# Turning k' with 128-row products against an identity instead of 64-row transposes

## The chip, the cores and the metric

One core of a Trainium2 chip. The sets of runs were on different chips, each with the kernel before in the same rounds. The metric is the device time of the whole kernel in microseconds, the median over several executions. The profile gives, for one execution, the span from the first to the last instruction, which is about 1.8 us shorter than the time. PE is the matrix engine (TensorE), PEld its weight loads, DVE VectorE, ACT ScalarE, POOL GpSimd.

## The reference

Linear attention with projected keys and values (8 batches, 8 heads, 1024 tokens, head width 64, projection to 64), followed by a gated feed-forward block on all 8192 tokens:

```python
k_proj = np.einsum('ks,bhsd->bhkd', E, k)
v_proj = np.einsum('ks,bhsd->bhkd', F, v)
scores = scale * np.matmul(q, k_proj.transpose(0, 1, 3, 2))
attn = softmax(scores)                      # over 64 projected keys
x = np.matmul(attn, v_proj)                 # gathered to (8192, 512)
g = x @ w_gate                              # 512 -> 1536
out = (g * sigmoid(g) * (x @ w_val)) @ w_out
```

## The kernel before

The feed-forward matmuls of batch b are the frame; the attention of the next batch is put into slots between them. In the profiles gps, vps and yps are the PSUM tiles of its gate, value and output products, kvp holds the projected k and v, kTp the turned k', sc the scores; `64*128` behind MATMUL or LDWEIGHTS is the tile of the PE array, rows times columns, that the instruction uses. The change touches one small stage: the projected k of a batch, k' (64 rows of projected keys, 8 heads x 64), comes out of PSUM into `ks`, is turned so that the head width lies on partitions, and is written into the block-diagonal `BD` from which the scores are computed.

```python
def u_KV(b, what="kv", hs=(0, H), at="a"):
    ...                                   # t[0:64] = E k, t[64:128] = F v
    if "k" in what:
        if (b, "s") not in kvp:
            kvp[b, "s"] = aw.tile([KP, H, D], BF16, name="ks", tag="ks")
        nc.scalar.copy(out=kvp[b, "s"][:, h0:h1], in_=t[0:64, h0:h1])
    ...

def u_KT(b, at="a", prs=(0, NPAIR)):
    ks = kvp[b, "s"]
    t = bank(at, [P, NPAIR, KP], BF16, "kTp")
    for pr in range(*prs):                # four pairs of heads
        nc.tensor.transpose(
            out=t[:, pr, :],
            in_=ks[:, 2 * pr : 2 * pr + 2, :].rearrange("p h d -> p (h d)"),
            identity=ident_bf[:KP, :KP],
        )
    bd = BD[b % 2][:].rearrange("p (a c) k -> p a c k", c=2)
    for c in range(2):
        src = t[64 * c : 64 * c + 64, slice(*prs)]
        nc.vector.tensor_copy(out=bd[0:64, slice(*prs), c, 0:64], in_=src)
        nc.vector.tensor_copy(out=bd[64:128, slice(*prs), c, 64:128], in_=src)
```

Each of batches 1 to 7 has one such visit of four transposes, in the middle of the feed-forward matmuls of the batch ahead of it. Batch 0 has two visits of two, in the opening, where nothing else is there to be computed yet:

```python
u_KV(0, "k", (0, 4), at="y"); warm(1)
u_T(0, 0, "a", act)
u_KT(0, at="v", prs=(0, 2))
...
u_S(0, 0, "g"); u_R(0, 0); u_N(0, 0)       # scores, sums, scaling (on POOL)
load_w_gv(1, 2, (1,))                      # weight loads, issued by POOL in this order
...                                        # the second half of k', more scores and scalings
load_w_gv(2, 4)                            # later weights, behind the scalings on POOL
```

The softmax here doesn't subtract the row's maximum and nothing guards it: scores larger than these inputs give would overflow.

## Time and profile before

| | before |
|---|---|
| time | 571.42 us, median of 3 (571.02 to 571.66) |
| span of the profiled run | 569.4 us |
| PE busy | 562.6 us, 99% |
| DVE busy | 335.2 us, 59% |
| PE's waits from 40 us on | none |

PE carries the kernel. Since its instructions overlap, busy time does not tell how densely they stand; what counts is the distance from one start to the next.

### The profile page before, as it was taken

To read this page: it belongs to the slowest core of one execution; us is meant where nothing else is said; L and a number is where in the kernel's file an instruction comes from. 1 tells how busy PE (TensorE), PEld (TensorE's weight loads), DVE (VectorE), ACT (ScalarE), POOL (GpSimd) and SP (SyncE) were. 2 spreads that over 40 slices of the span, in tenths; PEclk is the share of its full clock that TensorE was granted. 3 is DMA by queue.
4 is the path that set the end of the run, shared out by engine and by line. 5 is a ranking of instruction groups with operands and counts; after the bars stand their busy time and mean duration, and the time that the engine had idled before them with its cause. 6 is when DMAs were issued, how large, how long until landed. Compare 5 with 4: busy or idle time off the path is not lost.

```text
span 569.4 us, 7879 instructions
## 1 busy us (share of the span) xinstructions
PE 562.6 (99%) x2939; PEld 266.7 (47%) x2939; DVE 335.2 (59%) x577; ACT 236.8 (42%) x417; POOL 109.1 (19%) x122
## 2 busy tenths in 40 slices
PE   8999999999999999999999999999999999999997
PEld 5654444444444444444444444444444444444444
DVE  4776664766476655666466655666546665545550
ACT  4565442454435433443435434354343543443222
POOL 6742250124002400124002230023100220000000
PEclk9999999999999999999999999999999999999999
DMA  9999979829903696039931399105990213010002
GB/s 211 179 199 198 167 131 201 141 60 205 198 18 75 108 177 141 37 56 158 189 79 38 75 178 207 41 20 104 191 185 20 57 38 75 37 38 37 20 37 94
DMA packets 111143, 62.91 MB, mean 110 GB/s; under 512 B 64256, under 2 KB 102400, under 8 KB 111104
## 3 DMA queue, kind: packets, MB, share of 16 engines
q0 software_dynamic: 42800, 29.36, 36.3%
q1 hardware_dynamic: 67392, 31.46, 25.6%
q10 hardware_dynamic: 912, 1.57, 0.9%
q8 instruction: 23, 0.38, 0.3%
q14 instruction: 16, 0.13, 0.1%
HBM read 60.29 MB, written 16.78 MB: 135 GB/s over the span
## 4 chain that ended last, share of the span: by engine, by line
PE 92%; DMA 3%; DVE 2%; POOL 1%; ACT 1%; issue 0%; ACTq 0%; DVEq 0%; POOLq 0%
PE yps L362 29%; PE vps L324 28%; PE gps L324 27%; PE kvp L149 3%; PE sc L229 2%; PE pv L287 2%; DMA wv<-in_moe_w_val_dram 2%; DMA kraw<-in_k_dram 1%; DVE zz L244 1%; POOL AA L260 0%; POOL wg L117 0%; DVE hT L348 0%; ACT xT L137 0%; DVE s L343 0%; PE kTp L174 0%
## 5 line engine op out<-in xcount | busy, mean ns | idle before, releaser
L343 DVE SCALAR_TENSOR_TENSOR s<-th,gps 128x512 f32<-128x512 f32 x192 | 130.5, 679 | 143.1 <-ACT th L336 143.0
L324 PE MATMUL gps<-xT,wg 128*128 128x512 bf16 (+1 forms) x776 | 197.8, 377 | 0.6 <-DMA wg<-in_moe_w_gate_dram 0.4
L324 PE MATMUL vps<-xT,wv 128*128 128x512 bf16 (+1 forms) x776 | 197.5, 377 | 0.1
L362 PE MATMUL yps<-wo,hT 128*128 128x512 bf16 (+1 forms) x780 | 194.5, 376 | 0.0
L336 ACT ACTIVATE th<-gps 128x512 f32<-128x512 f32 x192 | 114.6, 597 | 157.9 <-PE gps L324 156.4
L348 DVE TENSOR_TENSOR hT<-s,vps 128x512 bf16<-128x512 f32 x192 | 132.0, 688 | 20.0
L260 POOL TENSOR_TENSOR AAd<-ee,rr 128x512 bf16<-128x512 f32 x56 | 58.3, 1041 | 343.3 <-issue 157.2
L362 PEld LDWEIGHTS <-hT 128*128 128x128 bf16 x780 | 76.2, 98 | 89.9
L324 PEld LDWEIGHTS <-wv 128*128 128x128 bf16 x776 | 73.9, 98 | 83.9 <-issue 3.3
L324 PEld LDWEIGHTS <-wg 128*128 128x128 bf16 x776 | 73.9, 98 | 82.1 <-issue 1.0
L372 ACT ACTIVATE ysb<-yps 128x512 f32<-128x512 f32 (+1 forms) x65 | 38.4, 591 | 76.7 <-PE yps L362 76.7
L137 ACT CAST xT<-pv 128x512 bf16<-128x512 f32 x63 | 36.6, 585 | 51.0 <-PE pv L287 50.1
L244 DVE TENSOR_REDUCE zz<-ee 128x8 f32<-128x512 f32 x64 | 43.4, 679 | 21.8 <-ACT ee L233 21.8
L233 ACT ACTIVATE ee<-sc 128x512 f32<-128x512 f32 x64 | 37.9, 595 | 23.6 <-PE sc L229 22.3
L229 PEld LDWEIGHTS <-qTd 128*128 128x128 bf16 x224 | 17.2, 98 | 13.2
L287 PE MATMUL pv<-AT,BDV 128*128 128x512 bf16 x60 | 22.4, 379 | 0.0
L229 PE MATMUL sc<-BD,qTd 128*128 128x128 bf16 x224 | 21.6, 219 | 0.0
L137 DVE CAST BDV<-kvp 64x256 bf16<-64x256 f32 x14 | 6.0, 426 | 20.0 <-ACT ks L159 17.8
L246 DVE RECIPROCAL rr<-zz 128x8 f32<-128x8 f32 x64 | 13.0, 203 | 7.4 <-DVE zz L244 1.4
L149 PE MATMUL kvp<-vb,FT 128*64 128x512 bf16 (+2 forms) x80 | 15.6, 338 | 0.3 <-ACT BDV L137 0.3
L149 PE MATMUL kvp<-kb,ET 128*64 128x512 bf16 (+1 forms) x72 | 15.5, 357 | 0.5 <-DMA kb<-in_k_dram 0.3
L107 POOL DMA_DIRECT2D qb<-in_q_dram x17 | 15.6, 919 | 0.6 <-DMA wv<-in_moe_w_val_dram 0.6
(51 smaller groups left out, 126.3 us busy)
## 6 DMA issues: line engine op xcount, KB each, us to landing
out_dram<-ysb SPq DMA_DIRECT2D x63, 256.0 KB, 2.4
qb<-in_q_dram POOLq DMA_DIRECT2D x15, 512.0 KB, 18.2
kb<-in_k_dram POOLq DMA_DIRECT2D x7, 1024.0 KB, 11.0
vb<-in_v_dram POOLq DMA_DIRECT2D x7, 1024.0 KB, 14.4
wo<-in_moe_w_out_dram POOLq DMA_DIRECT2D x2, 768.0 KB, 21.8
wg<-in_moe_w_gate_dram POOLq DMA_DIRECT2D x5, 256.0 KB, 9.5
wv<-in_moe_w_val_dram POOLq DMA_DIRECT2D x5, 256.0 KB, 10.1
kraw<-in_k_dram ACTq DMA_DIRECT2D x2, 512.0 KB, 4.7
```

What stands on the lines that cost most here:

```text
L137: (nc.scalar.copy if eng is nc.scalar else eng.tensor_copy)(out=out, in_=in_)
L149: nc.tensor.matmul(out=t[lo : lo + 64, h0:h1].rearrange("p h d -> p (h d)"), lhsT=w[:, j, :], rhs=src[b][:, h0:h1, j, :], start=(j == 0), ...
L229: nc.tensor.matmul(out=ps[:, n, :], lhsT=t[:, n, :], rhs=BD[b % 2][:, 4 * g + n, :], start=True, stop=True)
L233: nc.scalar.activation(out=e[:].rearrange("p h j k -> p (h j k)"), in_=ps[:].rearrange("p a k -> p (a k)"), func=AF.Exp, scale=scale,)
L244: nc.vector.reduce_sum(out=z[:], in_=e[:], axis=AX.X)
L260: eng.tensor_tensor(out=a.rearrange("p j h k -> p h j k"), in0=ee.pop((b, u))[:], in1=rr.pop((b, u))[:].unsqueeze(3).to_broadcast([P, 4, 2 ...
L324: nc.tensor.matmul(out=ps[:, ts], lhsT=(wg, wv)[w][:, kt, f * P : (f + 1) * P], rhs=x[:, kt, ts], start=(kt == 0), stop=(kt == NKT - 1),)
L336: nc.scalar.activation(out=th[:], in_=ps[:], func=AF.Tanh, scale=0.5)
L343: nc.vector.scalar_tensor_tensor(out=s1[:], in0=th[:], scalar=1.0, in1=g[:], op0=ALU.add, op1=ALU.mult)
L348: nc.vector.tensor_tensor(out=hT[c][:, f, :], in0=s1[:], in1=ps[:], op=ALU.mult)
L362: nc.tensor.matmul(out=yy[c][:, cs], lhsT=hT[c][:, f, i * P : (i + 1) * P], rhs=wo[:, f, cs], start=(f == 0), stop=(f == NFT - 1),)
L372: nc.scalar.activation(out=ysb[:, cs], in_=yy[c][:, cs], func=AF.Copy, scale=0.5)
```

## The change

The intent: take the 64-row operation out of the stream of 128-row ones. `ks` gets 128 rows, of which the lower 64 are zero, and the turn becomes an ordinary product with an identity, which writes fp32.

```diff
+    ks = [const.tile([P, H, D], BF16, name=f"ks{i}") for i in range(2)]
...
-            if (b, "s") not in kvp:
-                kvp[b, "s"] = aw.tile([KP, H, D], BF16, name="ks", tag="ks")
-            nc.scalar.copy(out=kvp[b, "s"][:, h0:h1], in_=t[0:64, h0:h1])
+            nc.scalar.copy(out=ks[b % 2][0:64, h0:h1], in_=t[0:64, h0:h1])
...
-        t = bank(at, [P, NPAIR, KP], BF16, "kTp")
+        t = bank(at, [P, NPAIR, KP], FP32, "kTp")
         for pr in range(*prs):
-            nc.tensor.transpose(
+            nc.tensor.matmul(
                 out=t[:, pr, :],
-                in_=ks[:, 2 * pr : 2 * pr + 2, :].rearrange("p h d -> p (h d)"),
-                identity=ident_bf[:KP, :KP],
+                lhsT=ks[b % 2][:, 2 * pr : 2 * pr + 2, :].rearrange("p h d -> p (h d)"),
+                rhs=ident_bf[:, 0:KP],
+                start=True,
+                stop=True,
             )
...
         for i in range(2):
+            nc.vector.memset(ks[i][64:P], 0.0)
```

More of the change, by code (lines that the diff above doesn't have):

```diff
@@ L169, in u_KT @@
     def u_KT(b, at="a", prs=(0, NPAIR)):
-        ks = kvp[b, "s"]
-        t = bank(at, [P, NPAIR, KP], BF16, "kTp")
+        t = bank(at, [P, NPAIR, KP], FP32, "kTp")
         for pr in range(*prs):
-            nc.tensor.transpose(
+            nc.tensor.matmul(
                 out=t[:, pr, :],
-                in_=ks[:, 2 * pr : 2 * pr + 2, :].rearrange("p h d -> p (h d)"),
-                identity=ident_bf[:KP, :KP],
+                lhsT=ks[b % 2][:, 2 * pr : 2 * pr + 2, :].rearrange("p h d -> p (h d)"),
+                rhs=ident_bf[:, 0:KP],
+                start=True,
+                stop=True,
             )
```

## The prediction

> **What bounds the kernel now.** I read the page first, then the list of waits of the matrix engine, then the timeline of that engine and of its weight loads around one of the places that the diff touches, then the groups by shape and the timeline of the opening. The page's first block and its chain come first:
>
> ```profile
> PE 562.6 (99%) x2939; PEld 266.7 (47%) x2939; DVE 335.2 (59%) x577; ACT 236.8 (42%) x417; POOL 109.1 (19%) x122
> ...
> PE 92%; DMA 3%; DVE 2%; POOL 1%; ACT 1%; issue 0%; ACTq 0%; DVEq 0%; POOLq 0%
> ```
>
> PE is busy 99% of the 569.4 us span, and 92% of the chain that ended last is PE. A busy PE is not yet a PE at its peak, so I asked what it waits for: in the list of PE's own waits there are eight entries, 1.2 us at most, all in the first 33 us; from 40 us to the end the list is empty. The granted clock is 0.999. So after the opening the time is the sum of what PE takes for its instructions in order. Only two things can move it: a matmul's own spacing, or a pause between matmuls that the list of waits does not name. The second is what this change is after. The timeline of PE at batch 2 (start us, length us, engine, line, operation, tile, count):
>
> ```profile
> 101.26 1.03 PE L362 MATMUL yps<-wo,hT 128*128 128x512 bf16 x4
> 102.22 0.29 PE L174 MATMUL kTp<-ident_bf,ks 64*128 64x64 bf16 x4
> 102.44 1.04 PE L324 MATMUL gps<-xT,wg 128*128 128x512 bf16 x4
> 103.32 1.03 PE L324 MATMUL vps<-xT,wv 128*128 128x512 bf16 x4
> 104.18 1.03 PE L362 MATMUL yps<-wo,hT 128*128 128x512 bf16 x4
> 105.04 0.39 PE L229 MATMUL sc<-BD,qTd 128*128 128x128 bf16 x4
> 105.27 0.38 PE L324 MATMUL gps<-xT,wg 128*128 128x512 bf16 x1
> ```
>
> Read starts, not lengths, since lengths overlap. A block of four 512-column matmuls takes 0.86 us when 128-row work follows (103.32 to 104.18, 104.18 to 105.04). The block ahead of the transposes takes 0.96 (101.26 to 102.22). The weight loads of the same stretch show why:
>
> ```profile
> 102.22 0.17 PEld L174 LDWEIGHTS <-ks 64*128 64x128 bf16 x4 [0.42 <-issue]
> 102.44 0.55 PEld L324 LDWEIGHTS <-wg 128*128 128x128 bf16 x4
> 103.10 0.75 PEld L324 LDWEIGHTS <-wv 128*128 128x128 bf16 x4
> ...
> 104.83 0.42 PEld L229 LDWEIGHTS <-qTd 128*128 128x128 bf16 x4
> ```
>
> The score weights (tile 128*128) are loaded at 104.83, 0.21 us ahead of their matmul at 105.04. The ks weights (tile 64*128) are not loaded ahead, they start with their matmul at 102.22, and so do the wg weights after them, at 102.44. At each change of the array's tile the load-ahead is lost.
>
> **What the Trainium skill says.** TensorEngine Tiling (Array Packing), Key Properties: "Changing tiling mode (not just tile) drains the TensorE". The trace agrees: the pause stands at 64*128 and not at the score block. PSUM — Partial Sum Buffer, Specifications (TRN2): TensorE writes fp32, except that transposes write the input's type; VectorE takes 0.52 ns an element when both sides are 2-byte, otherwise 1.04. So the change of the tile from bf16 to fp32 is forced, and the trace agrees on what it costs: in the groups by shape, copies of 64x256 out of bf16 take 284 to 289 ns, out of fp32 426.
>
> ```profile
> L137 DVE CAST BDV<-kvp 64x256 bf16<-64x256 f32 x14 | 6.0, 426 | 20.0 <-ACT ks L159 17.8 <-PE kvp L149 2.2
> L183 DVE COPY BD<-kTp 64x256 bf16<-64x256 bf16 x14 | 4.0, 289 | 0.2
> L183 DVE COPY BD<-kTp 64x128 bf16<-64x128 bf16 x4 | 0.9, 222 | 0.1
> ```
>
> TensorE: Matmul & The Clock Gate, LDWEIGHTS: a load's time goes with its columns, not its rows. The trace has 95 ns for 64 rows of 128 columns and 98 ns for 128 rows, so the zero lower half costs nothing to load. Perfetto Trace Analysis, Transposes, advises a real transpose over a standard matmul; that speaks against the change, and the trace shows nothing for or against it.
>
> **The change part by part.** The instructions on PE stay equal in number and order; there is no extra matmul.
>
> 1. The seven steady visits (batches 1 to 7, four transposes each). Before, one visit costs, beyond plain blocks: 0.96 - 0.86 = 0.10 ahead of it, 102.22 to 102.44 = 0.22 for the four and the pause behind them, and 0.02 because the next block takes 0.88 (102.44 to 103.32) rather than 0.86. Sum 0.34 us. I read four more visits (159.82, 227.77, 363.68, 431.63 us): 0.96 ahead, 0.21 to 0.22 within, each. After, the four are 64-column matmuls with no change of tile. Inside the visit now, four starts lie within 0.29 - 0.19 = 0.10 us (0.19 is one's length in the groups), so 0.033 apart; four at that spacing take 0.13. The score block, 128 columns, runs at 0.055 (0.22 for four), the worst case. Saving 0.34 - 0.13 = 0.21 us a visit, at worst 0.12; by seven, 1.5 us, at worst 0.8. All of it lies on the path, since PE waits for nothing there.
>
> 2. The four copies out of that tile on DVE: 426 rather than about 287 ns, 0.14 x 4 = 0.56 us a visit, 3.9 us of DVE busy in all. They lie beside PE. At batch 2 they run from 102.63 to 103.83; DVE then sits idle 0.32 us until 104.15. After, they end near 104.4, the next two eviction steps come 0.25 late, and an idle of 0.53 us follows before the next reduction. The score matmuls that read BD started at 105.04 and would come about 0.2 sooner, at 104.84: 0.4 us to spare, the tightest of the visits (there the scores start 2.8 us behind kTp, at batch 3 3.7 us). No cost to the end.
>
> 3. Two memsets of 64x256 words on DVE, some 0.27 each by the BDV memset of the same width (272 ns). DVE sits idle 1.6 us for the first k load there. Hidden.
>
> 4. The opening, batch 0, where k' is turned in two halves. The first is on a chain through scores, exponential, sums, scaling:
>
> ```profile
> 9.48 0.23 PE L174 MATMUL kTp<-ident_bf,ks 64*128 64x64 bf16 x2
> ...
> 10.46 0.23 DVE L183 COPY BD<-kTp 64x128 bf16<-64x128 bf16 x1
> 10.55 0.34 PEld L229 LDWEIGHTS <-qT 128*128 128x128 bf16 x4
> 10.55 0.52 PE L229 MATMUL sc<-BD,qT 128*128 128x128 bf16 x4
> ```
>
> The last copy ends at 10.69, inside the score block, which therefore takes 0.52 and not 0.39. A copy of 64x128 is 222 ns; from fp32 I estimate 222 + 128 x (426 - 287)/256 = 290. Four: +0.27 us, less about 0.1 as the drain ahead of kTp goes. So +0.17 there. In the second half the neighbour ahead is a turn of F in the 64*128 tile, so there the change of tile only moves from behind to ahead of kTp, and the four copies push the copies of AT and qT behind them by 0.27. But the opening ends with PE ahead of its weights: blocks at 31.89 and 33.21 us waited 0.5 and 0.2 us for loads of wg and wv, and the chain there is a transfer of 10 us with the DMA engines at 90% and more. Up to 0.7 us of delay on PE vanishes in it; only if the loads, issued behind the scaling on POOL, come late too, is 0.2 to 0.3 paid. I take +0.15.
>
> Sum: -1.5 + 0.15, rounded down a little for spacing: -1.25 us. 571.42 - 1.25 = 570.2.
>
> **The rivals.** (a) The pause does not come from the 64-row tile but from transposing, or from the first matmul on a new bank. Against it: the 128-row transposes of q in the second half of batch 0 (34.09 to 34.31) take 0.22 for four, with no extra. Were it so, nothing is saved and the opening's cost stays: 571.4 to 571.7. (b) The score matmuls come to wait for the slower copies, 0.4 us to spare at batch 2 by my count; a miss of 0.2 at one visit costs 0.2. DVE at 59% busy does not become the bound. (c) The opening's delay goes through in full, to the weight loads: +0.5 at most, 570.5. (d) Pauses ahead of and behind kTp vanish wholly and 64-column matmuls run at their shortest: 0.24 by seven, 1.7 us: 569.7. (e) Plain matmuls are paced slower than transposes, as the score block: 570.8.
>
> **Range and chances.** From (d) with a little of chance to (e) with the opening's cost and the 0.6 us that three runs of before lie apart: 569.5 to 571.3. A gain of 2% would be 11.4 us; all kTp visits together cost 7 x 0.34 = 2.4 us, so that is out of reach, and so is a loss of 2%, which would take a wait of 1.6 us at every visit. Hence 0.99 for within 2%, 0.0 for faster, and 0.01 for slower, kept for what I have not thought of.
>
> **What would show it right or wrong.** The timeline at batch 2: kTp as tile 128*128, 0.86 from the block ahead, 0.11 to 0.14 for the four; their weights loaded 0.2 us ahead of the first; the issue wait gone from the list for that line (3.0 us over 7 visits now). Copies of 64x256 at some 426 ns and no new entry in PE's waits after 40 us. If kTp still starts 0.96 after its block, step 1 is wrong and (a) holds; if the visits shrink but the time does not, the opening took it: compare the start of the first block after 33 us. A prediction fails outright if a score block waits for BD by name.

## The result, and the profile after

The changed kernel takes 570.19 us (median of 6, 569.91 to 571.33) where the kernel before takes 571.47 us (median of 6 with those of the same rounds). The ratio is 0.9981, with a 95% interval from 0.9968 to 0.9994: about 0.2% faster, within 2%, and clear of 1. Such a ratio is the mean time of one kernel's runs over that of the other's of the same rounds, so it is not quite the ratio of the two medians. In means the gain is 1.10 us, in medians 1.28 us. That difference is already a sign of how finely this can be timed: single runs of one kernel lie 0.6 to 1.4 us apart.

The page of the changed kernel opens with this:

```profile
PE 561.2 (99%) x2939; PEld 266.8 (47%) x2939; DVE 339.9 (60%) x579; ACT 236.7 (42%) x417; POOL 109.1 (19%) x122
```

As many PE instructions as before, 2939, and two DVE instructions more, the memsets; DVE is 4.7 us busier. The timeline of PE at the same visit, batch 2, in the changed kernel (start us, length us, engine, line, operation, tile, count):

```profile
101.66 1.03 PE L365 MATMUL yps<-wo,hT 128*128 128x512 bf16 x4
102.53 0.28 PE L175 MATMUL kTp<-ident_bf,ks 128*128 128x64 bf16 x4
102.64 1.03 PE L327 MATMUL gps<-xT,wg 128*128 128x512 bf16 x4
103.50 1.03 PE L327 MATMUL vps<-xT,wv 128*128 128x512 bf16 x4
104.37 1.03 PE L365 MATMUL yps<-wo,hT 128*128 128x512 bf16 x4
105.23 0.39 PE L232 MATMUL sc<-BD,qTd 128*128 128x128 bf16 x4
```

The block ahead of kTp now takes 0.87 us from its start to the start of kTp (0.96 before), the four products take 0.11 us (0.22), the block behind them 0.86 (0.88). From the start of the yps block to the start of the next yps block it is 2.71 us, and it was 2.92. The timeline of the weight loads of the same stretch shows the cause:

```profile
101.45 0.75 PEld L365 LDWEIGHTS <-hT 128*128 128x128 bf16 x4
102.31 0.37 PEld L175 LDWEIGHTS <-ks 128*128 128x128 bf16 x4
102.61 0.56 PEld L327 LDWEIGHTS <-wg 128*128 128x128 bf16 x4
```

The first ks load now starts at 102.31, 0.22 us ahead of its product at 102.53, under the last matmul of the block before. No `issue` wait (time in which the engine waited for nothing that the profile shows) stands at this line any more; before, the seven visits had 3.0 us of them on PEld (which is not the same as PE time: most of such a wait lies beside a running matmul).

The groups by shape of the changed kernel, for the copies out of the turned tile (mean ns before the last bar):

```profile
L186 DVE CAST BD<-kTp 64x256 bf16<-64x256 f32 x14 | 5.9, 423 | 0.2
L186 DVE CAST BD<-kTp 64x128 bf16<-64x128 f32 x4 | 1.2, 289 | 0.1
```

They cost 423 and 289 ns where they cost 289 and 222 ns out of bf16. At batch 2 the four end 2.23 us behind the start of kTp and the score block starts 2.70 us behind it, so 0.47 us remain.

To split the gain by stage I take starts that both profiles share. From the last feed-forward block ahead of the first visit to the first one behind the seventh, the time was 376.32 us (from 55.53 to 431.85) and is 374.86 us (from 56.14 to 431.00): 1.46 us less, 0.21 us for each of seven visits. From there to the start of the last run of yps matmuls (554.51 and 553.65) it is 122.7 us in both. The rest of the difference lies ahead of 56 us and is of the other sign: in these two profiles the first visit's block came 0.61 us later. How much of that belongs to the change is the subject of half of the experiments.

### The profile page after: what moved, and what is told of

Read it like the earlier page. It is cut to its first block, busy times and chain, and to the rows that moved or that the text cites. A ratio compares the mean times of both kernels' runs of the same rounds, so it can differ in the third digit from the quotient of the medians.

```text
span 568.5 us, 7881 instructions
## 1 busy us (share of the span) xinstructions
PE 561.2 (99%) x2939; PEld 266.8 (47%) x2939; DVE 339.9 (60%) x579; ACT 236.7 (42%) x417; POOL 109.1 (19%) x122
## 4 chain that ended last, share of the span: by engine, by line
PE 92%; DMA 3%; POOL 2%; ACT 1%; DVE 1%; issue 0%; POOLq 0%; DVEq 0%
PE yps L365 29%; PE vps L327 28%; PE gps L327 27%; PE kvp L150 3%; PE sc L232 2%; PE pv L290 2%; DMA wv<-in_moe_w_val_dram 2%; DMA kb<-in_k_dram 2%; POOL AA L263 0%; DVE zz L247 0%; POOL wg L118 0%; ACT xT L138 0%; POOL qb L108 0%; POOL wv L118 0%; ACT th L339 0%
```

## The experiments

Theory: a 64-row operation among 128-row ones costs PE a fixed pause ahead of and behind it, because the load of the next weights is not done ahead across the change of tile; everything else that the change touches lies beside PE, but for the copies in the opening. Rivals: that the gain comes from product instead of transpose, or from the storage; that the pause grows with the number of transposes and not of tile changes; that the slower copies are not really hidden; and, for the opening, that its later end is only chance of when weights land.

Time differences below are between the means of the runs, against the kernel before in the same rounds.

| kernel | batches 1 to 7 | batch 0 | median us | mean against before, us |
|---|---|---|---|---|
| the change (three times) | 128-row product | same | 570.19, 570.35, 570.32 | -1.10, -1.04, -1.21 |
| e3_prod64 | 64-row product | same | 571.71 | +0.27 |
| e2b_t128_full | 128-row transpose, bf16 | same | 570.53 | -0.78 |
| e6_storage | 64-row transpose, bf16 | same | 571.41 | -0.01 |
| e4_split_before | as before, two visits of two | as before | 573.03 | +1.60 |
| e5_split_after | 128-row product, two visits of two | 128-row product | 569.87 | -1.50 |
| e8_copies_twice | 128-row product, copies twice | 128-row product | 574.39 | +2.58 |
| e1_open_old (twice) | 128-row product | 64-row transpose, bf16 | 569.87, 570.14 | -1.58, -1.23 |
| e9_open_t128 | 128-row product | 128-row transpose, bf16 | 570.31 | -1.24 |
| e10_open_copies_twice | 128-row product | 128-row product, copies twice | 573.25 | +1.74 |

All gave the right result.

### Rows or product: e3_prod64, e2b_t128_full and e6_storage

Product over the 64 rows that hold data, into fp32:

```diff
-                lhsT=ks[b % 2][:, 2 * pr : 2 * pr + 2, :].rearrange(...),
-                rhs=ident_bf[:, 0:KP],
+                lhsT=ks[b % 2][0:KP, 2 * pr : 2 * pr + 2, :].rearrange(...),
+                rhs=ident_bf[:KP, 0:KP],
```

> Products into an fp32 tile as in the change, but over the 64 rows that hold data. Theory (rows make the pause): 0.96 us ahead of kTp and 0.22 us within stay in every visit, and the opening's slower copies are paid without the gain: 571.5 to 572.1. Rival (product instead of transpose makes the gain): 570.2 as the change.

Transposes over 128 rows, into bf16. In transpose mode the check ahead of the chip takes only a whole permutation as the moving operand, so the identity is 128 x 128, and each transpose has 128 columns:

```diff
-        t = bank(at, [P, NPAIR, KP], FP32, "kTp")
+        t = bank(at, [P, NPAIR, P], BF16, "kTp")
-            nc.tensor.matmul(..., rhs=ident_bf[:, 0:KP], start=True, stop=True)
+            nc.tensor.transpose(..., identity=ident_bf[:])
-            src = t[64 * c : 64 * c + 64, slice(*prs)]
+            src = t[64 * c : 64 * c + 64, slice(*prs), 0:KP]
```

> Transposes stay, into a bf16 tile with fast copies, but over all 128 rows (identity 128 x 128, so 128 columns each). Theory (the pause belongs to the 64-row tile): kTp starts 0.86 us after its block, four take 0.22 us, a visit costs 0.22 instead of 0.34 us; 571.47 - 7 x 0.12 = 570.6, with nothing paid in the opening, range 570.3 to 570.9. Rival (the pause belongs to transposing): kTp still starts 0.96 us after its block, time 571.5 or more.

Storage alone (the two fixed tiles and memsets of the change, with the old transposes on rows 0 to 63 and the bf16 tile):

> Only the storage part of the change: ks in two fixed tiles of 128 rows with two memsets of the lower half; the transposes stay on 64 rows in bf16. Theory: nothing on the path, 571.3 to 571.7. Rival (the memsets on DVE delay the opening by their 0.5 us): 571.8 to 572.1.

Measured: 571.71, 570.53 and 571.41 us, each inside the range that the theory gave. The timelines of PE at batch 2 say it more sharply than the times. First the 64-row product (e3_prod64):

```profile
102.04 1.03 PE L365 MATMUL yps<-wo,hT 128*128 128x512 bf16 x4
103.00 0.29 PE L175 MATMUL kTp<-ident_bf,ks 64*128 64x64 bf16 x4
103.22 1.04 PE L327 MATMUL gps<-xT,wg 128*128 128x512 bf16 x4
```

Then the 128-row transpose (e2b_t128_full):

```profile
101.48 1.03 PE L363 MATMUL yps<-wo,hT 128*128 128x512 bf16 x4
102.34 0.39 PE L175 MATMUL kTp<-ident_bf,ks 128*128 128x128 bf16 x4
102.56 1.03 PE L325 MATMUL gps<-xT,wg 128*128 128x512 bf16 x4
```

A product on 64 rows has the whole old pause, 0.96 us ahead and 0.22 within; a transpose on 128 rows has none, 0.86 ahead, and its 0.22 within is what the four 128-column matmuls of the score block take too. So the rows decide, not the kind of operation. On PE the product is still the better of the two 128-row forms, because it may stop at 64 columns: 0.11 us for four instead of 0.22. That fits the 0.78 us that e2b_t128_full gains, though its copies are fast; the whole times do not tell the two forms apart (the intervals of the ratio, 0.9974 to 0.9999 and 0.9968 to 0.9994, overlap). e6_storage is the kernel before in time and in the timeline (0.96 and 0.22): the memsets and the storage are hidden.

Both kernels also have the pause at a place that the change leaves alone and that has no 64-row operation. The projections of k and v at batch 2 use 128 rows and 64 columns; before the change:

```profile
94.99 1.03 PE L324 MATMUL gps<-xT,wg 128*128 128x512 bf16 x4
95.95 0.40 PE L149 MATMUL kvp<-kb,ET 128*64 128x512 bf16 x1
```

The block ahead takes 0.96 us here too (and 95.39 to 96.35 after the change), and their first weights are loaded only at 95.95. So it is the change of tile, in rows or in columns, that goes with the pause.

### A fixed cost per change of tile: e4_split_before and e5_split_after

The kernel before, and the changed one, with each visit of batches 1 to 7 split into two visits of two, one slot apart:

```diff
-            put(32, u_KT, 1)
+            put(31, u_KT, 1, "a", (0, 2))
+            put(32, u_KT, 1, "a", (2, 4))
-            put(s0 + (11 if b == 2 else 3), u_KT, b)
+            put(s0 + (10 if b == 2 else 2), u_KT, b, "a", (0, 2))
+            put(s0 + (11 if b == 2 else 3), u_KT, b, "a", (2, 4))
```

> The kernel before, with the four transposes of each of batches 1 to 7 in two visits of two, one slot apart: the same instructions on PE, twice the changes of tile. Theory (a fixed pause of 0.34 - 0.13 = 0.21 us per visit, whatever stands in it): 7 more visits, 571.5 + 1.5 = 573.0, range 572.6 to 573.4. Rival (the pause grows with the transposes, not with the changes of tile): 571.5.

> The change with the same split into two visits of two. Theory (no tile is changed, so a visit has no fixed cost): 570.2, range 569.9 to 570.6. Rival (any stop of the running accumulation costs, whatever the tile): up to 571.7.

Measured: 573.03 us and 569.87 us. PE in e4_split_before at batch 2:

```profile
99.80 1.03 PE L324 MATMUL gps<-xT,wg 128*128 128x512 bf16 x4
100.76 0.23 PE L174 MATMUL kTp<-ident_bf,ks 64*128 64x64 bf16 x2
100.92 1.04 PE L324 MATMUL vps<-xT,wv 128*128 128x512 bf16 x4
101.79 1.03 PE L362 MATMUL yps<-wo,hT 128*128 128x512 bf16 x4
102.75 0.23 PE L174 MATMUL kTp<-ident_bf,ks 64*128 64x64 bf16 x2
102.91 1.04 PE L324 MATMUL gps<-xT,wg 128*128 128x512 bf16 x4
```

Both visits have their 0.96 us ahead, and each half takes 0.16 us for two transposes, not half of the 0.22 that four take. The seven visits more cost 1.60 us in the means, 0.23 us each, with the same PE instructions; the theory said 1.5. In the changed kernel the same split costs nothing on PE: 2 x 0.06 us instead of 0.11, the blocks ahead at 0.86 to 0.87. Its time came out 0.3 to 0.5 us below the three medians of the unsplit change, just under the expected range, and each of its runs (569.81 to 570.06) lies below each run of the change on the same chip (570.08 to 570.70). From the first block behind the wait for wv to the end both profiles take 534.6 to 534.7 us, so the difference lies in the opening, where that block starts at 33.46 us instead of 33.72. The opening's program is the same in both; why the weights landed earlier is not shown.

### How well the copies are hidden: e8_copies_twice

The four copies are made twice in batches 1 to 7 (the same values, written again):

```diff
-        for c in range(2):
+        for c in (0, 1, 0, 1) if b else (0, 1):
```

> The change with its four copies out of the fp32 tile made twice in batches 1 to 7 (same values written again). It measures how far the slower copies are from the path. Theory (they end 0.44 us ahead of the score block at batch 2 and about 1.3 us ahead at batches 3 to 7): the extra 4 x 0.43 = 1.73 us makes score blocks wait by name for BD, some 1.3 us at batch 2 and 0.3 to 0.5 at batches 3 to 7, none at batch 1: 570.2 + 1.3 + 5 x 0.4 = 573.5, range 572.5 to 574.5. Rival (DVE work of this size is hidden with room to spare): 570.2.

Measured: 574.39 us, inside the range and near its end. The list of PE's waits in it from 40 us on, which is empty before and after the change, has one line:

```profile
PE sc L232 <- DVE BD L186: 2.8, 7, 0.6
```

The waits are 1.4 us at batch 2 (the score matmuls that should start at 105.73 and go through stand at 106.33 and 107.16) and less at the others. So the slower copies of the change are hidden, but not with much to spare: 0.56 us a visit fit, another 1.73 us do not. By this count a kernel with the scores one block (0.86 us) nearer would have paid for the fp32 tile.

### The opening: e1_open_old, e9_open_t128 and e10_open_copies_twice

e1_open_old turns batch 0 in the old way, batches 1 to 7 in the new:

```diff
-        t = bank(at, [P, NPAIR, KP], FP32, "kTp")
+        t = bank(at, [P, NPAIR, KP], FP32 if b else BF16, "kTp")
         for pr in range(*prs):
+            src = ks[b % 2][:, 2 * pr : 2 * pr + 2, :].rearrange(...)
+            if b == 0:
+                nc.tensor.transpose(out=t[:, pr, :], in_=src[0:KP], identity=ident_bf[:KP, :KP])
+                continue
```

> Batch 0 turns k' with 64-row transposes into a bf16 tile as before; batches 1 to 7 use the products of the change. Theory (seven visits save 0.22 us each, the opening pays for its fp32 copies): 571.47 - 7 x 0.22 = 569.93, range 569.6 to 570.3; the first block after the last wait for wv starts at 33.2 us as before, not at 33.9. Rival (the later opening in the profile of the change is only a matter of when the weights happened to land): the same 570.2 as the change, with the block at 33.2 to 33.9 by chance.

Measured 569.87 us (569.48 to 570.12), in the expected range. The second half of the expectation fell: in its profile the first block behind the wait for wv starts at 33.69 us, not at 33.2. It starts at 33.66 in e6_storage as well, which has the opening of the kernel before but for two hidden memsets. So 33.21 in the profile of the kernel before is an early one. The profiles let the opening be taken apart. From the first kTp to the pair of scalings on POOL, behind which the later weight loads are issued, it is 7.02 to 7.03 us in the five profiles that turn batch 0 by 64-row transposes, and 7.28 to 7.35 us in the five that have the change's opening: the chain is about 0.27 us longer. The start of that kTp (9.48 to 9.88 us) and the landing of the weights (the block starts 14.6 to 15.4 us behind the first of those issues) vary more than this from profile to profile. So of the 0.61 us by which the first visit comes later in the two profiles above, about 0.27 belongs to the change, and the rest lies within that scatter.

e9_open_t128 has the 128-row transposes of e2b in batch 0 and the products elsewhere:

> Batch 0 turned by 128-row transposes into bf16 (fast copies and no change of tile), batches 1 to 7 by the products of the change. Theory (the opening's cost comes from its fp32 copies alone): as with the old opening, 569.8, range 569.5 to 570.1, and 0.3 below the change. Rival (the opening's cost is the order or storage of the change): 570.2.

> The change itself once more, beside the next three on the same chip: 570.2, range 569.9 to 570.6. Its first block after the last wait for wv starts later than in a kernel with the old opening on the same chip by 0.2 to 0.3 us.

Measured 570.31 us (569.69 to 570.55) beside the change at 570.35 us (570.08 to 570.70): e9 missed its range by 0.2 us, and the difference of the two is not resolved. Its profile has PE waiting for k loads (0.3 us) in the opening, and its block behind the wait for wv only at 34.15 us, later than in the change's own (33.72), which points to late loads rather than to its turn of k': its chain from kTp to POOL takes 7.09 us, nearly as short as the old one. The change's block is 0.44 us behind that of e4_split_before (33.28), which has the old opening on the same chip; 0.2 to 0.3 was expected.

To see whether a later chain in the opening reaches the end at all, e10_open_copies_twice makes the opening's copies twice, and e1_open_old and the change were run again beside it:

```diff
-        for c in range(2):
+        for c in (0, 1) if b else (0, 0, 1, 1):
```

> The change with its copies out of the fp32 tile made twice in batch 0 alone (same values): the opening's score chain comes 4 x 0.31 = 1.2 us later still. Theory (a later chain delays the issue of the weight loads on POOL and is paid at the end, less what PE waited for weights, 0.5 to 0.7 us): the POOL issue behind the scaling moves from 18.8 to about 20.1 us, time 570.3 + 0.6 to 1.3 = 570.9 to 571.6. Rival (the weights' landing is set by the transfers alone and swallows it): 570.3.

> The version with the old opening once more, beside the change on the same chip: 569.9, range 569.6 to 570.2.

> The change beside it: theory (its opening costs 0.2 to 0.5 us) 570.3, 0.2 to 0.5 above the version with the old opening; rival (no cost, only chance of the loads) equal within 0.15.

Measured: 573.25 us (572.31 to 575.33), 570.14 us (569.92 to 571.12) and 570.32 us (570.09 to 570.95). e10 lies 1.65 us above its expected range, but the direction is the theory's. The timeline of POOL at the weight loads in the change beside it (e0_third):

```profile
17.06 2.04 POOL L263 TENSOR_TENSOR AA<-ee,rr 128x512 bf16<-128x512 f32 x2 [1.90 <-ACT ee L236]
19.05 0.80 POOL L118 DMA_DIRECT2D wg<-in_moe_w_gate_dram  x1
```

and in e10_open_copies_twice:

```profile
19.44 2.04 POOL L263 TENSOR_TENSOR AA<-ee,rr 128x512 bf16<-128x512 f32 x2 [3.10 <-ACT ee L236]
21.43 0.81 POOL L118 DMA_DIRECT2D wg<-in_moe_w_gate_dram  x1
```

The copies of both halves add up on the chain: from the first kTp to these scalings it is 9.82 us in place of 7.28 (2.5 us more, where I had counted one half, 1.2 us), and the issue of the weight loads moves by 2.4 us. Of that, 1.9 us arrive at the first block behind the wait for wv (35.99 against 34.07) and 1.8 us in the time of the two profiled runs (572.31 against 570.48). In the means it is 2.95 us, but that is not all the chain's: the three runs of e10 at the lower clock lie highest, and the three at 1.000 lie 2.3 us above the change of the same rounds. Whether the longer opening brought the lower clock, no run shows. So most of a later chain reaches the end, since the loads are issued behind it and come later with it. Whether PE's wait for weights swallows the missing half microsecond is not told apart from the 0.8 us by which the landing varies.

What the change's own opening costs is then a matter of a few tenths. Its chain is about 0.27 us longer. Its eight slower copies are 8 x (289 - 222) = 0.54 us of DVE in the two halves together. By times: 0.27 us in e3_prod64, which has the pauses and the slower copies; 0.3 us as the 1.46 us that the visits give less the 1.12 us that the change gains on the mean of its three sets. Directly, the change against e1_open_old on the same chip: 0.18 us in the medians and 0.02 in the means, below the 0.2 to 0.5 that was expected; in these two profiles the old opening even has its block later (34.20 against 34.07). And e5_split_after, with the same opening as the change, pays nothing. I hold "between nothing and half a microsecond, about 0.3" for what the runs support; they do not settle it further, because the landing of the weights moves by as much from one build, chip and run to the next.

No version is clearly better than the change. The one with the old opening, e1_open_old, gains 1.58 and 1.23 us in its two sets where the change gains 1.04 to 1.21; its lead is of the size of the spread. e5_split_after leads by 0.46 us in the means of its one set, from an earlier landing of weights that nothing here shows to be lasting.

## Why the prediction was right

The time, 570.2 us predicted and 570.19 us measured, is nearer than its terms deserve, and that is luck: the terms add up to 1.35 us, 0.1 of which was taken off for a spacing that then came out no wider than assumed, and the opening's cost was set too low by about as much. By its steps:

1. The visits: right, and in the right size. Saving predicted 1.5 us, measured 1.46 us between shared starts. The spacing of the four products, estimated at 0.033 us from the old transposes, is 0.11 / 4, some 0.028 us. The mechanism, row tile and lost load-ahead, stood up to the experiment for each half of it: 64 rows keep the pause with a product, 128 rows lose it with a transpose, and twice the tile changes cost it twice.
2. The copies on DVE: right. Predicted 426 ns, measured 423. Predicted spare 0.4 us ahead of the scores at batch 2, measured 0.47. No wait of PE behind 40 us. e8 shows that the spare was real and small.
3. The memsets: right, e6_storage is 0.01 us from the kernel before.
4. The opening: the right sign, the reason partly wrong. I counted on PE's waits for weights (0.5 and 0.2 us) to swallow most of a later chain, and took +0.15 us. e10 shows that most of a later chain reaches the end (1.8 of 2.4 us in the profiled runs), because the weight loads are issued behind it. The change's chain is about 0.27 us longer, and its cost in time is about 0.3 us in place of 0.15, poorly resolved. That the copies of both halves add up on the chain, as e10 shows, was not in my sum either: it weighed each half alone.

Of the rivals, (a) is refuted by e2b_t128_full and e3_prod64, (b) did not happen but lay 0.47 us away, (c) is closer to what the opening does than the central case was, and (d) and (e) bracket the spacing: the visits gave 1.46 us between the 1.7 of (d) and the 0.8 of (e). The spacing of (e) is that of e2b_t128_full, which gains 0.78 us.

## What to carry to other kernels

Where PE is the bound and shows no waits, compare the starts of equal blocks: a block that takes 0.1 us longer than its equals marks a pause that no list of waits names, and here it stood at a change of the array's tile. If only a few small operations use fewer rows, pad their operands with zeros to the tile of their neighbours; here a weight load took 98 ns in place of 95, and the gain was about 0.2 us for each visit. Look first at what the wider form costs elsewhere, such as fp32 out of a product and copies half as slow again, and at how much the next reader of those copies can wait.

## What the Trainium skill lacked or had wrong

- TensorEngine Tiling (Array Packing), Key Properties, says that a change of tiling mode drains the engine, without a size. Here it costs 0.10 us ahead and about 0.1 us behind a visit, 0.21 us together (0.23 by e4_split_before), whether a transpose or a product is on 64 rows; ahead of the projections with tile 128*64 it is 0.10 us as well.
- Perfetto Trace Analysis, Transposes, asks for a transpose in place of a standard matmul. Here the 128-row product of 64 columns takes 0.11 us for four and the 128-row transpose, which needs the whole identity, 0.22 us; the kernel with products gains 1.0 to 1.2 us in the means, that with 128-row transposes 0.78 us. That comes of the columns: on the same 64 rows and columns, product and transpose both take 0.22 us. The price of the product is the fp32 tile.
- TensorE: Matmul & The Clock Gate, Back-to-back issue gap, gives 81 ns as the sustained spacing of 128-column matmuls with their weight loads. Here it is 0.22 / 4 = 55 ns, and about 28 ns at 64 columns (0.11 / 4), each with its own load of 128 x 128 weights. At 512 columns the page gives 131 ns, and here it is 0.86 / 4 = 215 ns. The 56 and 216 ns that the same passage gives for lone matmuls are what this trace shows with loads.
